# Row maxima of two heads at once: the low products in two row tiles of 64 rows, 24 steps ahead of the scores

## The chip, the cores and the metric

The kernel runs on one core of a Trainium2 chip. The metric is the device time of one execution in microseconds. An engine's own queue runs in order; PE is the matrix engine, with its weight loads shown apart as PEld, DVE the vector engine, ACT the scalar engine, POOL the general engine, SP a queue that only issues transfers.

## The reference

Attention with pooled queries, 8 batches of 8 heads, then a layer of 8 experts of which each token takes one:

```python
q_pool = q.reshape(B, H, S // factor, factor, D).mean(axis=3)          # 576 queries, D = 64
scores = scale * np.matmul(q_pool, k.transpose(0, 1, 3, 2))            # 576 x 1152
scores = scores - np.max(scores, axis=-1, keepdims=True)
attn = np.exp(scores)
attn = attn / (np.sum(attn, axis=-1, keepdims=True) + 1e-09)
attn_out = np.matmul(attn, v)
...
h = np.maximum(x[mask] @ w1[e], 0.0)
out[mask] = gate_w[mask, None] * eom[mask, e, None] * (h @ w2[e])
```

## The kernel before

Attention comes first and lasts up to some 1030 us; the experts follow. The heads go in 32 pairs (two heads of one batch). A value in float32 is kept as a high part, rounded to the form in which the matrix engine streams at full rate, and a low part, the rest. A product of queries and keys is then three products: high with high, low q with high k, and high q with low k. `qa` holds the high q in 64 rows and the low q in 64 rows below; `ka` holds the high k twice. One matmul of `ka` and `qa` thus gives the first two. `qb` and `kb` hold high q and low k in rows 0 to 63 and, in further rows, what the scores need of the row maxima; a matmul of these gives the third product.

**Scores and exponentials.** A step of the program is one chunk of 128 keys of one head: 18 steps for a pair, 576 in all. In a step the scores (`sps`, keys in the partitions, 576 queries in two halves; lines 394 and 396) are computed on PE, ACT takes their exponential twice (`ph` in float16, `p32`), and POOL or DVE makes the low part `pl`. Six steps later `av` (lines 425 to 427) multiplies with the values, mostly two chunks in every other step (`BURST`).

**Maxima.** The scores are shifted by the row maximum, which must be known earlier. So the same products are computed a second time, now with queries in the partitions (`mgen`, line 331): a pair has 1152 queries, 9 tiles of 128, of which tile 4 takes the end of head 0 and the start of head 1; each tile has three chunks of 384 keys. A chunk is two matmuls into one PSUM bank (`mp`), three for tile 4, whose third takes `kp` (low k of both heads, head 0 in rows 0 to 63, head 1 in rows 64 to 127) with `qd`, a weight matrix with zeros outside two blocks. DVE reduces each chunk to one column of `pm` (line 332). There are three banks, given out in turn (`psum`); routers and transposes use them too. After 5 and after 9 tiles the columns are reduced (`m9`), transposed on PE (line 366, in `rows`), split in high and low (lines 371 and 372) and sent by transfers on ACT's queue into `qb`.

**Order.** It is written out by hand: the loop over steps calls, in this order, what is left of the step before (`pendv`), the routers, the scores, the preparation of a later pair (`prep_at`), maxima, more preparation, `rows`, and `av`. Maxima advance 27 chunks in 18 steps, 1.5 in a step, and end `LEAD` = 18 steps before the scores that need them. The preparation (table `PREP`: loads, sums, high and low parts, transfers into `ka`, `kb`, `qa`, `qb`) is set out in thirds of a step. `prep_at` counts them from an offset of at most 9.

**Router.** Every fourth pair a batch is complete; its logits `lT` (32 rows) are transposed on PE, five times 32 by 32 (line 522 of this kernel).

Of the kernel before, what the change touches and what calls it, by code (L numbers as in the profile page):

```python
# [8 lines left out]
F32 = mybir.dt.float32  # L9
F32R = mybir.dt.float32r  # L10
# [5 lines left out]
ALU = mybir.AluOpType  # L16
AX = mybir.AxisListType
PSUM = bass.MemoryType.PSUM

LEAD = 18  # L20
L0 = 18
LS = 0
RI = 7
PREP0 = ((0, 'lk'), (6, 'qsum'), (10, 'kh', 0), (11, 'qh'), (12, 'kh', 1), (13, 'ql'), (14, 'kl'), (13, 'dq', 0), (14, 'dq', 1), (17, 'qd'), (21, 'sk', 0, 0), (24, 'sk', 0, 1), (27, 'sk', 1, 0), (30, 'sk', 1, 1), (23, 'dl', 0), (24, 'dl', 1),
        (53, 'lv'), (71, 'amax', 0), (74, 'amax', 1), (81, 'gmax'), (82, 'scale', 0), (85, 'scale', 1), (90, 'scale', 2), (93, 'vh', 0), (93, 'vs', 0), (96, 'vh', 1), (97, 'vl', 0), (100, 'vs', 1), (104, 'vl', 1))
# [24 lines left out]
NQ = 576  # L50
# [17 lines left out]
def attention(tc, qT, kT, vL, wg, keep, xrows, idscr, cum, pairs, setup, scat, init, exps):  # L68
    nc = tc.nc
    nb = len(pairs) // 4  # L70
    with ExitStack() as ctx:
# [16 lines left out]
        def psum(hold=False, name="tp"):  # L88

            while len(held) == 3:  # L90
                pop() if fill else pendv.pop(0)()
            k = next(i for i in banks if i not in held)
            free(k)
            if hold:
                held.add(k)
            x = ps_m.tile([128, 512], F32, name=name, tag=f"mp{k}")
            return (x, k) if hold else x
# [11 lines left out]
        for L, shape, name in ((KBs, [68, 2, S], "kb"), (KAs, [128, 2, S], "ka"), (QAs, [128, 2 * NQ + 64], "qa"), (QBs, [68, 2, NQ], "qb")):  # L109
            for i in order:  # L110
                L[i] = (lp if i == order[2] else ep).tile(shape, F32R, name=f"{name}{i}")
        QDs = [ep.tile([128, 128], F32R, name=f"qd{i}") for i in range(2)]
        for i in range(3):
            nc.gpsimd.memset(QAs[i].bitcast(F32)[:, NQ:NQ + 64], 0.0)
# [15 lines left out]
        def prep(n, table):  # L130
# [2 lines left out]
            b, hp = p  # L133
            ka, kb, qa, qb, vt = KAs[n % 3], KBs[n % 3], QAs[n % 3], QBs[n % 3], VTs[n % 2]
            sc = sm.tile([128, 2], F32, name="sc", bufs=4)
            states[n] = dict(ka=ka, kb=kb, qa=qa, qb=qb, vt=vt, sc=sc, p=p, n=n, qd=QDs[n % 2])
            kp = ld.tile([128, S], F32R, name=f"kp{n}", tag="kp", bufs=KPB)
            kpf = ld.tile([128, S], F32, name="kpf")
            states[n]['kp'] = kp
# [2 lines left out]
            xk = sq.tile([128, S], F32R, name=f"xk{n}", tag="xk")  # L142
            yq = sq.tile([128, NQ], F32R, name="yq")
            qs = yq.bitcast(F32)
            xq = sq.tile([128, NQ], F32R, name="xq")
            am = sm.tile([128, 2], F32, name="am")
            inv2 = sm.tile([128, 2], F32, name="inv2")
            gm = []
# [151 lines left out]
                out.setdefault(r, []).append(f)  # L300
            return out

        def mtile(t):

            if t < 4: return [(0, 128 * t)]
            if t == 4: return [(0, 512), (1, NQ)]
            return [(1, NQ + 64 + 64 + 128 * (t - 5))]

        def mgen():

            for n in range(len(pairs)):
                st = states[n]
                ka, kb, qa, qb = st['ka'], st['kb'], st['qa'], st['qb']
                qbf = qb.rearrange("p h n -> p (h n)")
                for t0, t1 in ((0, 5), (5, 9)):
                    nt = t1 - t0
                    pm = sm.tile([128, 16], F32, name="pm")
                    ch = [(t, c) for t in range(t0, t1) for c in range(3)]
                    for i, (t, c) in enumerate(ch):
                        mp = psum(name=f"mp{n}")[:, 0:384]  # L320
                        cs = slice(384 * c, 384 * c + 384)
                        ops = []
                        mt = mtile(t)
                        for (h, o) in mt:
                            ops.append((qa[:, o:o + 128], ka[:, h, cs]))
                            if len(mt) == 1:
                                ops.append((qb[0:66, h, 128 * t if h == 0 else 64 + 128 * (t - 5):][:, 0:128], kb[0:66, h, cs]))
                        if len(mt) == 2:
                            ops.append((st['qd'], st['kp'][:, cs]))
                        for j, (l, r) in enumerate(ops):  # L330
                            nc.tensor.matmul(mp, lhsT=l, rhs=r, start=j == 0, stop=j == len(ops) - 1)  # L331
                        nc.vector.tensor_reduce(out=pm[:, i:i + 1], in_=mp, axis=AX.X, op=ALU.max)  # L332
                        pop()
                        if i < len(ch) - 1:
                            yield
                    m9 = sm.tile([128, 5], F32, name="m9")

                    def ch0(m9=m9, pm=pm, nt=nt, t0=t0, t1=t1, qbf=qbf):
                        nc.vector.tensor_reduce(out=m9[:, 0:nt], in_=pm[:, 0:3 * nt].rearrange("p (t c) -> p t c", c=3), axis=AX.X, op=ALU.max)
                        pend_t.append((m9, nt, t0, t1, qbf, now[0]))  # L340
                    fill.append(ch0)
                    yield

        fill = []
# [2 lines left out]
        def pop(k=1):  # L347
            while k and fill:
                fill.pop(0)()
                k -= 1  # L350
# [9 lines left out]

        def rows(force=False):
            while pend_t and (force or now[0] >= pend_t[0][-1] + TLAG):
                m9, nt, t0, t1, qbf, _ = pend_t.pop(0)
                tp, tk = psum(True)
                tp = tp[0:nt, 0:128]
                nc.tensor.transpose(out=tp, in_=m9[:, 0:nt], identity=ident)
                mr = sm.tile([5, 2, 128], F32R, name="mr")[0:nt]
                c0 = 16.0 * SHIFT

                def split(tp=tp, tk=tk, mr=mr, qbf=qbf, t0=t0, t1=t1, nt=nt):  # L370
                    nc.vector.tensor_scalar(out=mr[:, 0], in0=tp, scalar1=c0, scalar2=None, op0=ALU.subtract)
                    nc.vector.scalar_tensor_tensor(out=mr[:, 1], in0=tp, scalar=c0, in1=mr.bitcast(F32)[:, 0], op0=ALU.subtract, op1=ALU.subtract)
                    free(tk)

                    def send():
                        for j in range(2):
                            dmaf(qbf[66 + j:67 + j, 128 * t0:128 * t1].rearrange("o (t n) -> o t n", n=128), mr[:, j], nc.scalar)
                    pendd.append((send, now[0]))
                if now[0] < 18:
                    split()  # L380
                else:
                    pendv.append(split)
# [238 lines left out]
        def adv(k, g, want):  # L621
            while pos[k] < want:
                next(g, None)
                pos[k] += 1
# [3 lines left out]
        def prep_at(s, ph):  # L628
            u = 3 * (s + SLEAD) + ph
            for n in range(max(u // 54 - 2, 0), min(u // 54 + 2, NP)):  # L630
                r = u - 54 * n + min(3 * (LEAD - 15), 2 * n)
                if r == 0:
                    preps[n] = prep(n, PREP if n > 1 else PREP0 if n else PREPF)
                if n in preps:
                    for f in preps[n].pop(r, ()):
                        f()

        E = mybir.EngineType
        with tc.manual_schedule(engines={E.PE, E.DVE, E.Activation, E.Pool}):
            for s in range(-SLEAD, 0):  # L640
                for ph in range(3):
                    prep_at(s, ph)
                if s == -RI:
                    for i in (1, 2):
                        dmaf(QBs[i][64:66], QBs[0][64:66])
                        dmaf(KBs[i][64:68], KBs[0][64:68])
                if s == 1 - SLEAD + INIT:
                    consts()
                if s == -3:
                    init(0)  # L650
                if s >= -int(L0):
                    adv('m', mg, int(1.5 * (s + 1 + L0)))
                    now[0] = s
                    sends()
                    pop(3)
                    rows()
            for s in range(18 * NP + 14):
                now[0] = s
                live = s < 18 * NP
                if s % 18 == 2 and 0 < s // 18 < 5:  # L660
                    with tc.issue_after(lastk[0].ins):
                        init(s // 18)
                sends()
                while pendv:
                    pendv.pop(0)()
                for r in routers:
                    if not s % 2 or not live or not r[1]:
                        r[1] = next(r[0], 0)
                pop()
                if live:  # L670
                    next(sg)
                prep_at(s, 0)
                mw = min(27 * NP, int(1.5 * (s + 1 + min(LEAD, L0 + LS * s))))
                if pos['m'] < mw:
                    adv('m', mg, pos['m'] + 1)
                prep_at(s, 1)
                adv('m', mg, mw)
                if s < 54 or s % 2 == 0:
                    rows()
                if pos['m'] == 27 * NP:  # L680
                    pop(2)
                j = s - ALAG
                for _ in range(BURST.get(j % 18, 0) if 0 <= j < 18 * NP else 0):
                    next(ag)
                prep_at(s, 2)
                if not live:
                    pop(3)
            pop(99)
            for r in routers:
                for _ in r[0]: pass  # L690
# [512 lines left out]
```

## Time and profile before

| | |
|---|---|
| median of 2 runs | 1527.74 us (1527.46 to 1528.02) |
| profiled execution | 1531.21 us, span from first to last instruction 1529.5 us |
| mean granted clock of the matrix engine | 0.987 |
| PE / PEld busy | 1485.5 / 1347.8 us |
| ACT / DVE / POOL busy | 1123.0 / 1106.9 / 1005.6 us |
| matmuls of the maxima (L331) | 960 of ka, 768 of kb, 96 of kp |
| reduces of the maxima (L332) | 864 of 551 ns |

Busy time of PE is the union of matmuls that overlap, each with its whole latency; the cost of one in a stream is the distance between starts, which the timeline shows. An idle time has behind it the engine and the line that is thought to have ended it. A shape such as 66*128 is rows by columns of the weights.

### The profile page before, as it was taken

Reading aid. Unit: us, or ns where it says so; the run is one execution under the profiler, and the core shown is the slowest. Engines: PE = TensorE matmul, PEld = TensorE weight load, DVE = VectorE, ACT = ScalarE, POOL = GpSimd, SP = SyncE. Lnnn points to the kernel's source line nnn. Section 1 sums busy time; section 2 is a strip of 40 time slices with the busy share of each in tenths; the row PEclk is TensorE's granted clock in tenths of the full one; section 3 lists DMA queues with packets and bytes.
Section 4 is the critical chain, followed back from the end, with each engine's and each line's share of the span. In section 5 each row is a group of like instructions: output and inputs, shape, how many; then the busy total and the mean of one; then the engine's idle time right before and its main releaser. Section 6 shows DMA issues by size and latency. Waiting matters only on the chain. (4 is left out here: it accounts for less than half of the span.)

```text
span 1529.5 us, 40884 instructions
## 1 busy us (share of the span) xinstructions
PE 1485.5 (97%) x15838; PEld 1347.8 (88%) x15838; DVE 1106.9 (72%) x2339; ACT 1123.0 (73%) x1949; POOL 1005.6 (66%) x889
## 2 busy tenths in 40 slices
PE   7999999999999999999999999979999999999998
PEld 6999999999999999999999899967888888888875
DVE  7677777776786777677777777647777777777762
ACT  5888888887888888888888888865565565565552
POOL 4887898788878888889878988766233233333210
PEclk9999999999999999999999999989999999999999
DMA  5577566665675566656765676065836666544550
GB/s 168 135 193 188 134 153 172 164 150 133 160 171 155 134 158 167 162 133 156 176 154 152 146 176 161 19 241 164 319 106 231 233 216 224 203 151 163 179 188 35
DMA packets 91984, 253.35 MB, mean 166 GB/s; under 512 B 12714, under 2 KB 16954, under 8 KB 91778
## 3 DMA queue, kind: packets, MB, share of 16 engines
q1 hardware_dynamic: 81194, 228.93, 53.5%
q0 software_dynamic: 9152, 20.85, 3.9%
q8 instruction: 129, 2.11, 0.6%
q10 hardware_dynamic: 1440, 0.89, 0.2%
q14 instruction: 69, 0.57, 0.1%
HBM read 164.23 MB, written 23.02 MB: 122 GB/s over the span
## 5 line engine op out<-in xcount | busy, mean ns | idle before, releaser
L332 DVE TENSOR_REDUCE pm<-mp 128x1 f32<-128x384 f32 x864 | 453.1, 551 | 219.5 <-PE mp L331 218.5
L410 POOL TENSOR_TENSOR pl<-p,ph 128x576 f16<-128x576 f32 x383 | 490.4, 1286 | 148.7 <-ACT ph L409 116.0
L408 ACT ACTIVATE p<-sps 128x576 f32<-128x576 f32 x383 | 250.7, 655 | 98.6 <-PE sps L396 58.8
L331 PE MATMUL mp<-ka,qa 128*128 128x384 f32 x960 | 315.1, 344 | 0.0
L425 PEld LDWEIGHTS <-ph 128*128 128x128 f16 x2880 | 263.2, 97 | 40.0 <-issue 28.9
L425 PE MATMUL av<-vt,ph 128*128 128x65 f16 x2880 | 296.4, 194 | 0.1
L426 PE MATMUL av<-vt,ph 128*128 128x64 f16 x2880 | 294.2, 195 | 0.0
L427 PE MATMUL av<-vt,pl 128*128 128x65 f16 x2880 | 293.3, 193 | 0.0
L394 PE MATMUL sps<-qa,ka 128*128 128x288 f32 x1152 | 279.8, 325 | 13.4 <-DVE pl L404 6.6
L426 PEld LDWEIGHTS <-ph 128*128 128x128 f16 x2880 | 265.9, 97 | 0.8
L427 PEld LDWEIGHTS <-pl 128*128 128x128 f16 x2880 | 266.1, 99 | 0.0
L331 PE MATMUL mp<-kb,qb 66*128 66x384 f32 x768 | 260.9, 340 | 0.9 <-DVE kb L205 0.6
L409 ACT ACTIVATE ph<-sps 128x576 f16<-128x576 f32 x383 | 249.4, 651 | 0.0
L396 PE MATMUL sps<-qb,kb 68*128 68x288 f32 x1152 | 248.6, 298 | 0.0
L905 PE MATMUL hps<-x,w1h 128*128 128x512 f32 (+1 forms) x704 | 233.3, 393 | 6.7 <-DVE x L889 4.2
L394 PEld LDWEIGHTS sps<-qa,ka 128*128 128x128 f32 x1152 | 185.0, 192 | 18.2 <-ACT ph L409 9.0
L396 PEld LDWEIGHTS sps<-qb,kb 68*128 68x128 f32 x1152 | 187.4, 191 | 0.0
L331 PEld LDWEIGHTS mp<-ka,qa 128*128 128x128 f32 x960 | 178.7, 190 | 1.8 <-DVE pm L332 1.5
L907 ACT COPY hs<-hps 128x512 f32<-128x512 f32 (+1 forms) x88 | 49.1, 558 | 174.0 <-PE hps L905 174.0
L905 PE MATMUL hps<-x,w1l 128*128 128x256 f32 (+1 forms) x704 | 167.0, 279 | 0.0
L404 DVE TENSOR_TENSOR pl<-sps,ph 128x576 f16<-128x576 f32 x193 | 145.9, 756 | 20.1 <-ACT sps L401 18.3
L400 ACT ACTIVATE ph<-sps 128x576 f16<-128x576 f32 x193 | 126.4, 655 | 41.1 <-PE sps L396 30.8
(231 smaller groups left out, 2948.0 us busy)
## 6 DMA issues: line engine op xcount, KB each, us to landing
ka<-xk SPq DMA_DIRECT2D x120, 288.0 KB
raw1b<-in_w_dram SPq DMA_DIRECT2D x24, 1024.0 KB
raw2b<-in_w_dram SPq DMA_DIRECT2D x24, 1024.0 KB
raw1a<-in_w_dram SPq DMA_DIRECT2D x22, 1024.0 KB
raw2a<-in_w_dram SPq DMA_DIRECT2D x22, 1024.0 KB
vp<-in_vL_dram SPq DMA_DIRECT2D x32, 576.0 KB
qp<-in_qT_dram SPq DMA_DIRECT2D x31, 576.0 KB
kpf<-in_kT_dram SPq DMA_DIRECT2D x31, 576.0 KB
```

The costliest lines, as they stand in the source:

```text
L331: nc.tensor.matmul(mp, lhsT=l, rhs=r, start=j == 0, stop=j == len(ops) - 1)
L332: nc.vector.tensor_reduce(out=pm[:, i:i + 1], in_=mp, axis=AX.X, op=ALU.max)
L394: nc.tensor.matmul(sps[:, j, 0:288], lhsT=ka[:, h, ks], rhs=qa[:, o + 288 * j:o + 288 * j + 288], start=True, stop=False)
L396: nc.tensor.matmul(sps[:, j, 0:288], lhsT=kb[:, h, ks], rhs=qb[:, h, 288 * j:288 * j + 288], start=False, stop=True)
L404: nc.vector.tensor_tensor(out=pl.rearrange("p (j n) -> p j n", j=2), in0=x, in1=ph2, op=ALU.subtract)
L408: nc.scalar.activation(out=p32.rearrange("p (j n) -> p j n", j=2), in_=x, func=AF.Exp, scale=1.0 / 16)
L409: e_ = nc.scalar.activation(out=ph2, in_=x, func=AF.Exp, scale=1.0 / 16)
L410: nc.gpsimd.tensor_tensor(out=pl, in0=p32, in1=ph, op=ALU.subtract)
L425: nc.tensor.matmul(av_[:, qb, 0:65], lhsT=hi, rhs=vt[:, h, c, 0:65], start=c == 0 and qb == 0, stop=False)
L426: nc.tensor.matmul(av_[:, qb, 0:64], lhsT=hi, rhs=vt[:, h, c, 66:130], start=False, stop=False)
L427: nc.tensor.matmul(av_[:, qb, 0:65], lhsT=lo, rhs=vt[:, h, c, 0:65], start=False, stop=c == NC - 1 and qb == 4)
L905: nc.tensor.matmul(hp[:, f, 0:n], lhsT=W1[l][g][:, c, fs], rhs=d['x'][:, c, 0:n], start=c == 0 and l == 0, stop=c == 3 and l == 0)
```

## The change

From the second pair on, the maxima of tile t of head 0 and tile t of head 1 are computed together, into two banks: first the product of `ka` and `qa` for head 0, then for head 1, each of 128 rows; then the product of high q and low k for head 0 from rows 0 to 63 of `xq` and `kp`, and for head 1 from rows 64 to 127 of the same tiles. These two are tiles of 64 rows by 128 columns at row 0 and row 64. `xq`, high q of both heads as `kp` has low k, becomes double buffered. Tile 4 stays as it was. The first pair keeps the old form.

A pair has then 15 events (12 double tiles and 3 single ones of tile 4). A table, `EVENTS`, sets the steps: from 24 before the pair's scores to 7 before, one event in a step and none at the 7th, 11th and 17th; the single ones stand 3rd, 9th and 15th of the 18. The second pair has a table of its own. The 9 columns of maxima are closed once for a pair: one reduce, one transpose, two sends. The preparation up to the transfers starts earlier (`OFFA`, 21 thirds of a step at most), the preparation of the values keeps its place.

```diff
-LEAD = 18
 L0 = 18
-LS = 0
+OFFA = (0, 2, 14, 20, 21)
+EVENTS = tuple(-24 + i for i in range(18) if i not in (6, 10, 16))
+EVENT1 = (-18, -17, -16, -15, -14, -13, -13, -12, -11, -11, -10, -9, -9, -8, -7)
...
+        XQs = [sq.tile([128, NQ], F32R, name=f"xq{i}") for i in range(2)]
...
+                for i in range(15):
+                    t, c = (4, i // 5) if i % 5 == 2 else divmod(i - (i + 2) // 5, 3)
+                    cs = cols[c]
+                    if t == 4:
                         mp = psum(name=f"mp{n}")[:, 0:384]
...
+                        both(mp, cs)
+                        reduce(pm, 12 + c, mp)
+                    else:
+                        o = (128 * t, 64 + 128 * t)
+                        mp = [psum(name=f"mp{n}")[:, 0:384] for _ in range(2)]
+                        for h in range(2):
+                            nc.tensor.matmul(mp[h], lhsT=qa[:, h * o1 + o[h]:h * o1 + o[h] + 128], rhs=ka[:, h, cs], start=True, stop=False)
+                        for h in range(2):
+                            r = slice(64 * h, 64 * h + 64)
+                            nc.tensor.matmul(mp[h], lhsT=xq[r, o[h]:o[h] + 128], rhs=kp[r, cs], start=False, stop=True)
+                        for h in range(2):
+                            reduce(pm, 3 * (5 * h + t) + c, mp[h])
+                    if i == 14:
+                        closing(pm, 9, 0, qbf)
                     yield
...
-                r = u - 54 * n + min(3 * (LEAD - 15), 2 * n)
-                if r == 0:
+                ra, rv = u - 54 * n + OFFA[min(n, 4)], u - 54 * n + min(9, 2 * n)
+                if ra == 0:
                     preps[n] = prep(n, PREP if n > 1 else PREP0 if n else PREPF)
                 if n in preps:
-                    for f in preps[n].pop(r, ()):
-                        f()
+                    for r in (ra,) if ra < 50 else (rv,) if rv >= 50 else ():
+                        for f in preps[n].pop(r, ()):
+                            f()
...
+        steps = [18 * n + e for n in range(1, NP) for e in (EVENTS if n > 1 else EVENT1)]
...
-                mw = min(27 * NP, int(1.5 * (s + 1 + min(LEAD, L0 + LS * s))))
-                if pos['m'] < mw:
+                for _ in range(steps.count(s)):
                     adv('m', mg, pos['m'] + 1)
                 prep_at(s, 1)
-                adv('m', mg, mw)
```

On PE, two steps of the 18th pair's scores before (numbers behind a name tell the buffers apart; `sps` are scores, `mp` maxima, the weighted sums `av` begin with the last row):

```order
L394 MATMUL sps_12214<-qa_123,ka_120 128x288 x2
L396 MATMUL sps_12214<-qb_126,kb_117 128x288 x2
L331 MATMUL mp_12225<-ka_121,qa_124 128x384
L331 MATMUL mp_12225<-kb_118,qb_127 128x384
L331 MATMUL mp_12229<-ka_121,qa_124 128x384
L331 MATMUL mp_12229<-kb_118,qb_127 128x384
L394 MATMUL sps_12240<-qa_123,ka_120 128x288 x2
L396 MATMUL sps_12240<-qb_126,kb_117 128x288 x2
L331 MATMUL mp_12249<-ka_121,qa_124 128x384
L331 MATMUL mp_12249<-kb_118,qb_127 128x384
L425 LDWEIGHTS ph
```

The same two steps of the changed kernel, whose lines 421 and 423 are the scores, 361 the full products, 364 the products of 64 rows and 452 the weighted sums:

```order
L421 MATMUL sps_12073<-qa_123,ka_120 128x288 x2
L423 MATMUL sps_12073<-qb_126,kb_117 128x288 x2
L361 MATMUL mp_12084<-ka_121,qa_124 128x384
L361 MATMUL mp_12085<-ka_121,qa_124 128x384
L364 MATMUL mp_12084<-kp_11080,xq_129 128x384
L364 MATMUL mp_12085<-kp_11080,xq_129 128x384
L421 MATMUL sps_12102<-qa_123,ka_120 128x288 x2
L423 MATMUL sps_12102<-qb_126,kb_117 128x288 x2
L361 MATMUL mp_12111<-ka_121,qa_124 128x384
L361 MATMUL mp_12112<-ka_121,qa_124 128x384
L364 MATMUL mp_12111<-kp_11080,xq_129 128x384
L364 MATMUL mp_12112<-kp_11080,xq_129 128x384
```

Three chunks into three banks, one after the other, became four chunks into two banks at a time; behind the first group stand scores, behind the second the weighted sums.

On PE, where the maxima of a pair are transposed, before (line 366, at the end of the first five tiles, ahead of the weighted sums):

```order
L331 MATMUL mp_12490<-ka_121,qa_124 128x384
L331 MATMUL mp_12490<-kb_118,qb_127 128x384
L366 MATMUL tp<-ident,m_12388 5x128
L425 LDWEIGHTS ph
L425 MATMUL av_12253<-vt_140,ph 128x65
```

And now (line 393, once for a pair, behind a single tile of the next pair, which is `both` in line 319):

```order
L319 MATMUL mp_12416<-ka_122,qa_125 128x384 x2
L319 MATMUL mp_12416<-kp_11744,qd_132 128x384
L393 MATMUL tp<-ident,m_12319 9x128
L452 LDWEIGHTS ph
L452 MATMUL av_12119<-vt_142,ph 128x65
```

The transpose has 9 rows instead of 5 and 4; the second one of a pair is gone.

More of the change, by code (lines that the diff above doesn't have):

```diff
@@ L135, in prep @@
             sc = sm.tile([128, 2], F32, name="sc", bufs=4)
-            states[n] = dict(ka=ka, kb=kb, qa=qa, qb=qb, vt=vt, sc=sc, p=p, n=n, qd=QDs[n % 2])
+            xq = XQs[n % 2]
+            states[n] = dict(ka=ka, kb=kb, qa=qa, qb=qb, vt=vt, sc=sc, p=p, n=n, qd=QDs[n % 2], xq=xq)
             kp = ld.tile([128, S], F32R, name=f"kp{n}", tag="kp", bufs=KPB)
@@ L144, in prep @@
             qs = yq.bitcast(F32)
-            xq = sq.tile([128, NQ], F32R, name="xq")
             am = sm.tile([128, 2], F32, name="am")
@@ L301, in prep, with reduce, closing, ch0 @@
             return out
[L303 to L307, printed above, removed]
+        def reduce(pm, i, mp):
+            nc.vector.tensor_reduce(out=pm[:, i:i + 1], in_=mp, axis=AX.X, op=ALU.max)
+            pop()
+        def closing(pm, nt, t0, qbf):
+            m9 = sm.tile([128, 9], F32, name="m9")
+            def ch0():
+                nc.vector.tensor_reduce(out=m9[:, 0:nt], in_=pm[:, 0:3 * nt].rearrange("p (t c) -> p t c", c=3), axis=AX.X, op=ALU.max)
+                pend_t.append((m9, nt, t0, qbf, now[0]))
+            fill.append(ch0)
+        def group(mp, *ops):
+            for j, (l, r) in enumerate(ops):
+                nc.tensor.matmul(mp, lhsT=l, rhs=r, start=j == 0, stop=j == len(ops) - 1)
         def mgen():
@@ L312, in mgen @@
                 st = states[n]
-                ka, kb, qa, qb = st['ka'], st['kb'], st['qa'], st['qb']
+                ka, kb, qa, qb, kp, xq = (st[x] for x in ('ka', 'kb', 'qa', 'qb', 'kp', 'xq'))
                 qbf = qb.rearrange("p h n -> p (h n)")
[L315 to L319, printed above, removed]
-                        mp = psum(name=f"mp{n}")[:, 0:384]
[L321 to L341, printed above, removed]
@@ new lines, in mgen, with both @@
+                o1 = NQ + 64
+                def both(mp, cs):
+                    group(mp, (qa[:, 512:640], ka[:, 0, cs]), (qa[:, NQ:NQ + 128], ka[:, 1, cs]), (st['qd'], kp[:, cs]))
+                cols = [slice(384 * c, 384 * c + 384) for c in range(3)]
+                if n == 0:
+                    for t0, t1 in ((0, 5), (5, 9)):
+                        pm = sm.tile([128, 32], F32, name="pm")
+                        for i in range(3 * (t1 - t0)):
+                            t, cs = t0 + i // 3, cols[i % 3]
+                            mp = psum(name="mp0")[:, 0:384]
+                            if t == 4:
+                                both(mp, cs)
+                            else:
+                                h, o = (0, 128 * t) if t < 4 else (1, 64 + 128 * (t - 5))
+                                group(mp, (qa[:, h * o1 + o:h * o1 + o + 128], ka[:, h, cs]), (qb[0:66, h, o:o + 128], kb[0:66, h, cs]))
+                            reduce(pm, i, mp)
+                            if i < 3 * (t1 - t0) - 1:
+                                yield
+                        closing(pm, t1 - t0, t0, qbf)
+                        yield
+                    continue
@@ new lines, in mgen @@
+                pm = sm.tile([128, 32], F32, name="pm")
+                for i in range(15):
+                    t, c = (4, i // 5) if i % 5 == 2 else divmod(i - (i + 2) // 5, 3)
+                    cs = cols[c]
+                    if t == 4:
+                        mp = psum(name=f"mp{n}")[:, 0:384]
+                        both(mp, cs)
+                        reduce(pm, 12 + c, mp)
+                    else:
+                        o = (128 * t, 64 + 128 * t)
[9 more added lines that the diff above has]
+                        closing(pm, 9, 0, qbf)
@@ L362, in rows @@
             while pend_t and (force or now[0] >= pend_t[0][-1] + TLAG):
-                m9, nt, t0, t1, qbf, _ = pend_t.pop(0)
+                m9, nt, t0, qbf, _ = pend_t.pop(0)
                 tp, tk = psum(True)
@@ L366, in rows, with split @@
                 nc.tensor.transpose(out=tp, in_=m9[:, 0:nt], identity=ident)
-                mr = sm.tile([5, 2, 128], F32R, name="mr")[0:nt]
+                mr = sm.tile([9, 2, 128], F32R, name="mr")[0:nt]
                 c0 = 16.0 * SHIFT
-                def split(tp=tp, tk=tk, mr=mr, qbf=qbf, t0=t0, t1=t1, nt=nt):
+                def split(tp=tp, tk=tk, mr=mr, qbf=qbf, t0=t0, t1=t0 + nt):
                     nc.vector.tensor_scalar(out=mr[:, 0], in0=tp, scalar1=c0, scalar2=None, op0=ALU.subtract)
@@ L672, in attention @@
                 prep_at(s, 0)
-                mw = min(27 * NP, int(1.5 * (s + 1 + min(LEAD, L0 + LS * s))))
-                if pos['m'] < mw:
+                for _ in range(steps.count(s)):
                     adv('m', mg, pos['m'] + 1)
                 prep_at(s, 1)
-                adv('m', mg, mw)
                 if s < 54 or s % 2 == 0:
                     rows()
-                if pos['m'] == 27 * NP:
+                if s > steps[-1]:
                     pop(2)
```

## The prediction, made before the changed kernel ran

> **What bounds the kernel now.** I read the page first (engine table and clock), then the table by stretches of time, then the groups of the maxima, and last the timeline of the matrix engine around single matmuls. The page:
>
> ```profile
> PE 1485.5 (97%) x15838; PEld 1347.8 (88%) x15838; DVE 1106.9 (72%) x2339; ACT 1123.0 (73%) x1949; POOL 1005.6 (66%) x889
> ...
> PEclk9999999999999999999999999989999999999999
> ```
>
> ```profile
> 400.00:600.00 200.00, 198.13 (x2703) 187.07 (x2702) 150.28 (x381) 170.13 (x315) 170.72 (x151) 1.00 0.60 151
> 600.00:800.00 200.00, 198.13 (x2696) 187.48 (x2693) 149.80 (x373) 170.41 (x316) 167.73 (x147) 1.00 0.64 158
> 950.00:986.00 36.00, 36.00 (x488) 34.30 (x487) 27.22 (x67) 29.79 (x55) 26.60 (x24) 1.00 0.17 45
> 986.00:1017.00 31.00, 26.31 (x402) 24.16 (x401) 9.74 (x22) 26.18 (x46) 25.09 (x19) 0.89 0.39 139
> ```
>
> The columns after the length are busy us of PE, PEld, DVE, ACT and POOL. In the attention's steady part PE is busy 198 of 200 us at full clock; ACT and POOL have 30 us in 200 to spare, DVE 50. In that stage whatever PE needs more or less goes into the time one for one. From 986 us on there are no maxima left, and PE is idle for 5 of 31 us.
>
> The share of the change:
>
> ```profile
> L331 PE MATMUL mp<-ka,qa 128*128 128x384 f32 x960 | 315.1, 344 | 0.0
> L331 PE MATMUL mp<-kb,qb 66*128 66x384 f32 x768 | 260.9, 340 | 0.9 <-DVE kb L205 0.6 <-ACT kb L207 0.3
> L332 DVE TENSOR_REDUCE pm<-mp 128x1 f32<-128x384 f32 x864 | 453.1, 551 | 219.5 <-PE mp L331 218.5
> L366 PE MATMUL tp<-ident,m 128*5 128x128 f32 x64 | 17.5, 273 | 0.9 <-DVE m L339 0.7
> L394 PE MATMUL sps<-qa,ka 128*128 128x288 f32 x1152 | 279.8, 325 | 13.4 <-DVE pl L404 6.6 <-ACT ph L409 6.5
> L522 PE MATMUL tp<-ident,lT 32*128 32x32 f32 x40 | 4.1, 227 | 0.3 <-DVE lT L501 0.3
> ```
>
> The means (344, 340 ns) are latencies and overlap. What a matmul costs in a stream is the distance from start to start, which the timeline of PE gives (start, duration):
>
> ```profile
> 502.60 0.34 PE L331 MATMUL mp<-ka,qa 128*128 128x384 f32 x1
> 502.77 0.34 PE L331 MATMUL mp<-kb,qb 66*128 66x384 f32 x1
> 502.94 0.34 PE L331 MATMUL mp<-ka,qa 128*128 128x384 f32 x1
> 503.12 0.34 PE L331 MATMUL mp<-kb,qb 66*128 66x384 f32 x1
> 503.29 0.42 PE L394 MATMUL sps<-qa,ka 128*128 128x288 f32 x2
> ```
>
> Two maxima tiles are four matmuls from 502.60 to 503.29: 0.69 us, **0.173 us each**. The product with 66 rows costs as much as the one with 128. That is what the change aims at: 12 double tiles in each of 31 pairs, 372 in all, whose two low products are to run side by side.
>
> **What going into a row tile costs.** This kernel has one place with a matmul of few rows, the 32-row transposes of L522 (shape 32*128), between maxima and scores:
>
> ```profile
> 301.40 0.34 PE L331 MATMUL mp<-ka,qa 128*128 128x384 f32 x1
> 301.57 0.33 PE L331 MATMUL mp<-kb,qb 66*128 66x384 f32 x1
> 301.83 0.49 PE L522 MATMUL tp<-ident,lT 32*128 32x32 f32 x5
> 302.26 0.53 PE L394 MATMUL sps<-qa,ka 128*128 128x288 f32 x2
> 302.63 0.43 PE L396 MATMUL sps<-qb,kb 68*128 68x288 f32 x2
> ```
>
> ```profile
> 301.40 0.19 PEld L331 LDWEIGHTS mp<-kb,qb 66*128 66x128 f32 x1
> 301.83 0.38 PEld L522 LDWEIGHTS tp<-ident,lT 32*128 32x128 f32 x5 [0.24 <-DVE r L435]
> 302.26 0.30 PEld L394 LDWEIGHTS sps<-qa,ka 128*128 128x128 f32 x2
> ```
>
> Elsewhere the weights of the next matmul are loaded while the last one streams (the load at 301.40 starts with the matmul at 301.40). Here the load and the first 32-row matmul start together at 301.83, **0.26 us** after the last full matmul and not 0.173. The five transposes pass at (0.49 - 0.227) / 4 = 0.066 us, so the last starts at 302.09; the scores' load begins 0.17 us later, again with its matmul, and the two L394 take 0.53 us where the pair at 503.29 took 0.42: **0.11 us** of weight load in the open. I read this as the array running empty before it changes to a row tile and before it changes back. The release named in brackets (DVE, L435) is a guess of the trace; the 0.26 speaks against it, since a wait for another engine would not fit the end of the stream so well.
>
> Of the 40 transposes most take 222 ns, the first of a group 244:
>
> ```profile
> L522 PE MATMUL tp<-ident,lT x40: 221/222/244, 178.1 to 1024.0; 32*128 32x32 f32 x40
> ```
>
> A narrow tile the other way shows nothing of the kind:
>
> ```profile
> 309.39 0.34 PE L331 MATMUL mp<-kb,qb 66*128 66x384 f32 x1
> 309.58 0.27 PE L366 MATMUL tp<-ident,m 128*4 128x128 f32 x1
> 309.68 0.19 PE L425 MATMUL av<-vt,ph 128*128 128x65 f16 x1
> 309.71 0.19 PE L426 MATMUL av<-vt,ph 128*128 128x64 f16 x1
> ```
>
> Four columns of weights come 0.19 us after the matmul before. So it is rows, not columns, that the 0.26 belongs to. The Trainium skill, "TensorEngine Tiling (Array Packing)", section Key Properties, says that a change of tiling mode, not just of the tile, drains the engine: the 0.26 agrees with it, and if L366's narrow load counts as a mode of that page, its 0.19 doesn't.
>
> **The sum for one double tile.** Before: 0.69. After: full product of head 0, 0.173; head 1, then 0.26 until the first 64-row load; that load in the open, 0.11; the second 64-row matmul behind the first by a distance d; 0.26 until the load of what follows; its load in the open, 0.11 before scores or a router's float32 matmul, 0.03 before the weighted sums (the distance 309.68 to 309.71). By the table of steps 9 of the 12 double tiles of a pair stand in odd steps, where scores or a router follow, and 3 in even steps, where the weighted sums follow.
>
> The load going in isn't in the trace: 0.02 if it hides as L522's did (0.244 - 0.222), 0.11 if it is like L394's. It is a float32 load of 128 columns for a plain product, as L394's, so 0.11. For d the bounds are 0 (both at once) and 0.173 (not side by side at all); the only two row-tiled matmuls in a row, L522's, are 0.066 apart, and I take that.
>
> - followed by float32: 0.173 + 0.26 + 0.11 + 0.066 + 0.26 + 0.11 = 0.98, that is +0.29
> - followed by float16: 0.90, that is +0.21
> - mean (9 x 0.29 + 3 x 0.21) / 12 = +0.27; times 372: **+100 us**
>
> The Trainium skill, "TensorE: Matmul & The Clock Gate", Part 3 (the mechanism), puts concurrent row tiles some 4 ns apart. By it d is 0.004 and the term 0.062 x 372 = 23 us smaller; no run shown here has two row tiles at once.
>
> **The other parts.** One closing reduce, one transpose and two sends for a pair instead of two, two and four. Of these only the transpose is on PE: 31 x 0.10 (309.58 to 309.68) = -3 us; the DVE and ACT parts lie beside PE. The maxima end 24 steps before the scores and not 18, so the last 24 steps have none. The row 986 to 1017 shows that such steps don't wait for PE, so taking maxima out of six more steps gives nothing back, while their work (6 x 1.5 tiles x 2 x 0.173) joins earlier steps: +3 us. A longer PE lets ACT and DVE get ahead, so part of the 13.4 us that L394 waited for them goes: -5 us, half or less since some of it stands after 986. The prep's loads come earlier by up to four steps, and the first double tile follows the last loads of qa by about four steps instead of six (about 1.7 us a step: 558 steps up to 986 us); the transfers run beside PE and I cost this at nothing. If one were late, PE would wait for it once a pair, 31 times; 1 us each would be 31 us. The three single tiles (head 0's end with head 1's start, three full matmuls) keep their cost.
>
> Sum: 100 - 3 + 3 - 5 = +95 us. The profiled execution took 1531.21 us with a span of 1529.5; the runs' median is 1527.74, 0.2% less, so the sum is simply put on the median: 1622 us, 6% slower. Bounds: with the first load hidden and d = 0 a double tile costs +0.13 or +0.05, mean 0.11, 42 us, with the other parts 1565; with d = 0.173 it is +0.38, 140 us, 1663. A few us of difference are nothing against the 2% (31 us) that counts here as no change.
>
> **The rivals.**
>
> *No drain for tiles of 64 rows (faster).* L522 has 32 rows and is a transpose; the L366 row shows that a partial tile need not cost anything. Then a double tile is 3 x 0.173 plus d: 0.52 to 0.59 instead of 0.69, -0.10 to -0.17, 38 to 64 us off: 1464 to 1490, say 1478. ACT and POOL, at 170 of 200, would let a pair shrink that far. The point from which it decides: in and out together may cost 0.10 us before the gain is gone; L522 shows about 0.39 (twice 0.09 and twice 0.11). Against it stands that row; I give 0.13. The same Trainium skill page on tiling, section Theoretical Speedup, puts up to a factor of two on contractions of 64 rows or less; the rival is what that would bring here.
>
> *Drain, but no load in the open.* If both loads are done while the array empties, a double tile is 0.173 + 0.26 + 0.03 + 0.26 = 0.72, +0.03, 12 us: 1540. For it: L522's first load cost 0.02. Against it: the 0.11 at L394 on the way out. The same band holds the case that the 64-row matmuls are not placed as tiles at all and run like full ones: no switch, four times 0.173, no change. Together 0.07.
>
> *Banks.* A double tile takes two of the three banks of the maxima at once, and a reduce holds one for 0.55 us. Three times in a pair two double tiles stand with only scores between (the first place shown ahead): four banks within some 1.5 us of PE. If DVE is then behind, PE waits up to one reduce, 93 x 0.55 = 51 us on top of the forecast: 1673. Against it: DVE has 50 us in 200 free, and its 219.5 us idle at L332 are waits for PE. It decides when the first reduce ends over 1.5 us after its tile began. 0.08.
>
> **How the numbers follow.** Forecast (switches drain, loads partly in the open, side by side or nearly) 0.72; banks on top 0.08; loads hidden or no tiles 0.07; no drain 0.13. Slower by over 2% (above 1558): 0.72 + 0.08 = 0.80; within 2%: 0.07; faster: 0.13. The range leaves out the fast rival and the far end of the banks, and takes in the bounds 1565 and 1663 with most of the way down to the second rival: 1545 to 1662.
>
> **What the changed profile would show.** The first 64-row matmul starts 0.26 us after head 1's full product, its load with it: right; 0.17: the drain is absent. The distance of the two 64-row matmuls gives d: under 0.03 they are loaded and run side by side, at 0.17 they aren't. The scores behind a double tile start with their load, as at 302.26, and their first pair takes 0.53. DVE, ACT and POOL are less busy in each 200 us of the attention (ACT about 154 for 170), and PE's stretch of 200 us remains full. PE waiting at the maxima's line for DVE's reduces would be the rival of the banks. The forecast is wrong if row tiles of 64 switch without emptying the array.

## The result, and the profile after

The changed kernel takes 1800.07 us (median of 2 runs, 1795.76 to 1804.38) against 1527.74: 1.178 times the time before, interval 1.166 to 1.190. The direction was forecast, the size was not: +272 us where +95 stood.

The page of the changed kernel (line 306 is the reduce of the maxima, 361 the full products of a double tile, 364 the products of 64 rows):

```profile
PE 1637.2 (91%) x15807; PEld 1334.9 (74%) x15807; DVE 1089.8 (61%) x2246; ACT 1121.0 (62%) x1949; POOL 1002.6 (56%) x889
PEclk9898899999899988889999998989899999999999
L306 DVE TENSOR_REDUCE pm<-mp 128x1 f32<-128x384 f32 x864 | 444.5, 552 | 504.5 <-PE mp L364 492.4
L361 PE MATMUL mp<-ka,qa 128*128 128x384 f32 x744 | 219.4, 367 | 108.4 <-DMA qa<-yq 70.1
L364 PE MATMUL mp<-kp,xq 64*128 64x384 f32 x744 | 173.9, 464 | 0.0
```

PE is no longer full, and its clock has dips. The table by stretches of time (busy us of PE, PEld, DVE, ACT, POOL, then the granted clock) says the same of the steady part:

```profile
400.00:600.00 200.00, 178.38 (x2081) 142.85 (x2081) 112.62 (x273) 131.68 (x245) 130.86 (x114) 0.92 0.52 124
600.00:800.00 200.00, 176.12 (x1954) 142.01 (x1951) 106.46 (x259) 124.38 (x232) 124.65 (x110) 0.87 0.47 110
```

No other engine has come near its limit; all are idler than before. So PE waits, and the list of who waited for whom (us in total, times, longest) names what for:

```profile
PE mp L361 <- DMA qa<-yq: 70.1, 33, 4.5
PE mp L361 <- DMA kb<-kp: 27.0, 16, 3.3
```

97 us of waits for transfers, once or twice a pair. The maxima of the double tiles don't read `kb`; its transfers stand in the same queue, between the two into `qa`, and the list names a wait after the transfer that seems to have ended it. One pair's first events on PE's timeline, and the clock in three stretches around them:

```profile
486.69 0.43 PE L421 MATMUL sps<-qa,ka 128*128 128x288 f32 x2
486.95 0.43 PE L423 MATMUL sps<-qb,kb 68*128 68x288 f32 x2
490.59 0.41 PE L361 MATMUL mp<-ka,qa 128*128 128x384 f32 x1 [3.21 <-DMA qa<-yq]
492.45 0.66 PE L361 MATMUL mp<-ka,qa 128*128 128x384 f32 x1 [1.45 <-DMA qa<-yq]
493.04 0.69 PE L364 MATMUL mp<-kp,xq 64*128 64x384 f32 x2
```

```profile
480.00:486.00 6.00, 6.00 (x89) 5.06 (x87) 4.04 (x9) 4.94 (x12) 4.66 (x6) 1.00 0.98 214
486.00:498.00 12.00, 7.34 (x52) 5.30 (x52) 3.22 (x8) 4.09 (x8) 1.93 (x2) 0.72 0.53 132
498.00:520.00 22.00, 21.73 (x274) 17.69 (x275) 14.21 (x34) 16.85 (x29) 17.99 (x15) 1.00 0.28 71
```

Head 0's product waits 3.21 us, head 1's 1.45 more, and then the clock is low for a while: head 1's product of 384 columns, 0.34 us elsewhere, takes 0.66, and the two of 64 rows 0.69 instead of 0.44. This comes back with nearly every pair. Over the whole execution the mean clock is 0.940 where it was 0.987, so (1 - 0.940) x 1793.9 = 108 us worth of clock are missing instead of 20.

The queue SP shows when the data set out. The two transfers of low q into `qa`, before and after (start, duration of the issue):

```profile
485.67 0.54 SPq L126 DMA_DIRECT2D qa<-yq  x1
488.81 0.46 SPq L126 DMA_DIRECT2D qa<-yq  x1
```

```profile
483.91 0.46 SPq L128 DMA_DIRECT2D qa<-yq  x1
486.39 0.46 SPq L128 DMA_DIRECT2D qa<-yq  x1
```

The first of each two is head 0's, the second head 1's. Head 1's now goes out at 486.39, and PE reaches the event that needs both at 487.38 (490.59 - 3.21), behind the scores. Before, head 1's `qa` was first read by chunk 12 of its pair, eight steps after the maxima began; now the very first event reads both heads'.

The times of issue, of landing and of the first reader, as medians over the 31 pairs, say it for both halves. Before, head 0's transfer was issued 9.0 us ahead of its first reader and took 5.7 us to land; head 1's was issued 19.4 us ahead and took 4.1. Now PE reaches the first event 5.1 us after head 0's issue and 2.9 us after head 1's, and both take 6.6 us. So neither half is there in time: PE idles 63 us ahead of the first products of head 0 and 45 us ahead of those of head 1.

The tiles themselves, on the same timeline:

```profile
501.64 0.45 PE L364 MATMUL mp<-kp,xq 64*128 64x384 f32 x2
502.02 0.53 PE L421 MATMUL sps<-qa,ka 128*128 128x288 f32 x2
502.39 0.43 PE L423 MATMUL sps<-qb,kb 68*128 68x288 f32 x2
502.66 0.52 PE L361 MATMUL mp<-ka,qa 128*128 128x384 f32 x2
503.10 0.44 PE L364 MATMUL mp<-kp,xq 64*128 64x384 f32 x2
```

Two products of 64 rows together take 0.44 or 0.45 us, as long as a single one (0.44, shown below): they run side by side. Over all 372 double tiles the median distances from start to start are 0.268 us from head 1's full product to the first of 64 rows, 0.003 from it to the second, and 0.37 to what follows.

### The profile page after: what moved, and what is told of

It reads as the page before. It is cut to its first block, busy times and chain, and to the rows that moved or that the text cites. A ratio compares the mean times of both kernels' runs of the same rounds, so it can differ in the third digit from the quotient of the medians.

```text
span 1793.9 us, 40456 instructions
## 1 busy us (share of the span) xinstructions
PE 1637.2 (91%) x15807; PEld 1334.9 (74%) x15807; DVE 1089.8 (61%) x2246; ACT 1121.0 (62%) x1949; POOL 1002.6 (56%) x889
## 5 line engine op out<-in xcount | busy, mean ns | idle before, releaser
L306 DVE TENSOR_REDUCE pm<-mp 128x1 f32<-128x384 f32 x864 | 444.5, 552 | 504.5 <-PE mp L364 492.4
L361 PE MATMUL mp<-ka,qa 128*128 128x384 f32 x744 | 219.4, 367 | 108.4 <-DMA qa<-yq 70.1
L452 PE MATMUL av<-vt,ph 128*128 128x65 f16 x2880 | 316.9, 199 | 0.8 <-DVE xb L463 0.8
L453 PE MATMUL av<-vt,ph 128*128 128x64 f16 x2880 | 314.8, 200 | 0.0
L454 PE MATMUL av<-vt,pl 128*128 128x65 f16 x2880 | 314.0, 198 | 0.0
L421 PE MATMUL sps<-qa,ka 128*128 128x288 f32 x1152 | 304.4, 347 | 8.9 <-DVE pl L431 6.3
L452 PEld LDWEIGHTS <-ph 128*128 128x128 f16 x2880 | 274.2, 100 | 40.5 <-issue 32.1
L454 PEld LDWEIGHTS <-pl 128*128 128x128 f16 x2880 | 278.4, 102 | 0.0
L453 PEld LDWEIGHTS <-ph 128*128 128x128 f16 x2880 | 277.8, 101 | 0.7
L361 PEld LDWEIGHTS mp<-ka,qa 128*128 128x128 f32 x744 | 133.1, 201 | 128.4 <-issue 92.8
L364 PE MATMUL mp<-kp,xq 64*128 64x384 f32 x744 | 173.9, 464 | 0.0
```

The costliest lines, as they stand in the source:

```text
L361: nc.tensor.matmul(mp[h], lhsT=qa[:, h * o1 + o[h]:h * o1 + o[h] + 128], rhs=ka[:, h, cs], start=True, stop=False)
L364: nc.tensor.matmul(mp[h], lhsT=xq[r, o[h]:o[h] + 128], rhs=kp[r, cs], start=False, stop=True)
L421: nc.tensor.matmul(sps[:, j, 0:288], lhsT=ka[:, h, ks], rhs=qa[:, o + 288 * j:o + 288 * j + 288], start=True, stop=False)
L452: nc.tensor.matmul(av_[:, qb, 0:65], lhsT=hi, rhs=vt[:, h, c, 0:65], start=c == 0 and qb == 0, stop=False)
L453: nc.tensor.matmul(av_[:, qb, 0:64], lhsT=hi, rhs=vt[:, h, c, 66:130], start=False, stop=False)
L454: nc.tensor.matmul(av_[:, qb, 0:65], lhsT=lo, rhs=vt[:, h, c, 0:65], start=False, stop=c == NC - 1 and qb == 4)
```

## The experiments

Each was timed beside the kernel before on its chip (1529.8 to 1530.43 us there, 1527.74 for the result above); "us" are medians. All the numbers of theories in the expectations are from before the run.

**Preparation three steps earlier.**

```diff
-OFFA = (0, 2, 14, 20, 21)
+OFFA = (0, 2, 14, 26, 30)
```

> The changed kernel with the preparation of queries and keys nine thirds of a step earlier (three steps, OFFA 30 instead of 21 from the fifth pair on), row tiles and events as they are. Theory A (late transfers: PE waits some 100 us for qa, the gaps halve the clock for some 200 us, which costs some 90 us, and the row tiles themselves cost 85 us): the waits for qa go under 15 us, the mean clock returns to 0.98 or more, the time is about 1610 us. Theory B (the tiles of 64 rows make the array look idle and so halve the clock): the waits go, but the clock stays near 0.94 and the time near 1700 us.

Measured: 1645.42 us, ratio 1.078 (1.073 to 1.082), clock 0.988. What PE still waits for:

```profile
PE av L454 <- POOL pl L437: 11.4, 8, 5.4
...
PE mp L361 <- DMA qa<-yq: 6.0, 2, 4.5
```

The waits for `qa` went down to 6 us and the clock came back with 372 row tiles still in the program: theory B falls. It took 155 us off. The time is 35 us above theory A's; 11 of them are a new wait, for POOL, that the earlier preparation brings, and the rest stays open here.

**No row tiles, everything else as changed.**

```diff
-                            nc.tensor.matmul(mp[h], lhsT=xq[r, o[h]:o[h] + 128], rhs=kp[r, cs], start=False, stop=True)
+                            nc.tensor.matmul(mp[h], lhsT=qb[0:66, h, o[h]:o[h] + 128], rhs=kb[0:66, h, cs], start=False, stop=True)
```

> The changed kernel with its events and its preparation as they are, but the low products taken from kb and qb as full matmuls of 66 rows, so that no row tile is left in the maxima. Theory A: the waits for qa remain (90 us or more, now also for kb), the clock stays near 0.94, the time falls by the tiles' 85 us to about 1715 us. Theory B: the clock returns to 0.98, about 1630 us.

Measured: 1811.40 us, ratio 1.184 (1.180 to 1.188), clock 0.916.

```profile
PE mp L361 <- DMA qa<-yq: 95.1, 35, 5.5
PE mp L361 <- DMA kb<-kp: 46.2, 22, 5.4
```

Without a single row tile in the maxima the time is no better, and the clock is lower: the waits and the clock are not of the tiles. Theory A missed the time by 96 us. In these two lines the waits are 141 us for 97, and (1 - 0.916) x 1810.7 = 152 us worth of clock are missing for 108, so the tiles' price didn't come off. A PE that is quicker reaches the same transfers earlier; but the low products now also need `kb`, which is issued last, and the run doesn't tell the two reasons apart.

**Both edits.** 

> Both edits: no row tiles, and the preparation nine thirds earlier. Both theories: no waits, full clock, about the time of the kernel before (1525 to 1535 us); against the run with early preparation alone the difference is the price of the row tiles, 85 us by theory A (372 tiles of 0.23 us).

Measured: 1614.54 us, ratio 1.057 (1.053 to 1.060). A miss for both theories: with neither tiles nor more than 7 us of waits for `qa` it is still 85 us above before. Against the first experiment the row tiles cost 31 us and not 85. Two waits are long; of the first the kernel before had none, of the second 6.6 us:

```profile
PE av L453 <- POOL pl L436: 16.9, 10, 6.5
PE sps L420 <- DVE pl L430: 14.4, 28, 1.1
```

**Events two steps later.**

```diff
-EVENTS = tuple(-24 + i for i in range(18) if i not in (6, 10, 16))
+EVENTS = tuple(-22 + i for i in range(18) if i not in (6, 10, 16))
```

> The changed kernel with the events two steps later (22 steps ahead of the scores instead of 24), preparation and row tiles as they are. Theory A: the transfers get 3.5 us more, which is about what PE waited in a pair, so most of the waits go (under 40 us), the clock is 0.97 or more, about 1630 us. Theory B: clock near 0.94, 1700 us or more.

Measured: 1764.46 us, ratio 1.153 (1.147 to 1.159), clock 0.956.

```profile
PE sps L423 <- DMA qb<-mr: 52.0, 27, 2.5
```

A miss for theory A in time (1630) and clock (0.97); the time alone would fit theory B, which the first two experiments exclude. The waits for `qa` are down to 2 us, and a new one took their place: the scores now wait for their own maxima (`mr` into `qb`). The events have no room to move later, since the maxima are sent only behind the last of them.

**Transfers of another pair.** To take the waits away without moving anything, the maxima read the `qa` of the pair before, which landed long ago; the shift of the scores then comes from other queries.

```diff
+                qa = states[max(n - 1, 0)]['qa']
```

> The changed kernel whose maxima read the qa of the pair before (which has long landed) instead of their own, so that their shift is that of another pair's queries; every instruction, its shape and its place stay. Theory A (late transfers and the clock behind them are all but the tiles' price): no waits for qa, half clock under 40 us, time 1528 + 85 for the tiles + some 10 at the start = 1615 to 1630 us. Rival C (the order of events itself costs steadily, since the two early runs without waits for qa still lay 85 us above theory): 1645 us or more.

Measured: 1626.29 us, ratio 1.062 (1.058 to 1.067), clock 0.990. The steady part:

```profile
400.00:600.00 200.00, 197.79 (x2475) 160.03 (x2474) 133.12 (x320) 156.36 (x289) 155.92 (x135) 1.00 0.59 141
```

PE is full again at full clock, and the time is in theory A's band, under rival C's. **The late `qa`, with all that follows from it, costs 1800 - 1626 = 174 us.**

**The same without row tiles.** Here qa, qb and kb are those of the pair before, and the low products have 66 rows as in the second experiment. 

> The same with qa, qb and kb of the pair before and full matmuls of 66 rows for the low products: the events' order alone, with neither row tiles nor late transfers. Theory A: 1530 to 1545 us. Rival C: 1570 us or more. The difference to the run with row tiles is the tiles' price: 85 us from the distances (372 x 0.23), or 30 to 40 if PE's extra time again hides other waits.

Measured: 1588.54 us, ratio 1.039 (1.033 to 1.045): above theory A, for rival C. The order of events costs some 58 us by itself in this run, so the fifth experiment's 96 us are not the 85 for tiles and 10 for the start that theory A put there. Part of the 58 can be named:

```profile
PE sps L423 <- DMA qb<-mr: 9.0, 7, 2.5
PE mp L362 <- DMA ka<-xk: 8.0, 7, 2.3
...
PE tp L393 <- DVE lT L528: 5.4, 20, 0.5
```

The tiles add 38 us to it, not the 85 of their distances, as was held possible. A quicker PE meets waits that a slower one doesn't: it idles 60 us here and 43 with the tiles. These 17 us are a part of the difference of 47; the rest isn't shown.

**Transfers into qa first.**

```diff
-(26, 'ql'), (29, 'qd'), (30, 'dl', 0), (32, 'dl', 1),
+(26, 'ql'), (29, 'qd'), (27, 'dl', 0), (28, 'dl', 1), (31, 'db', 0), (33, 'db', 1),
```

where `db` holds the transfers into `qb` and `kb` that stood in `dq` and `dl`. 

> The changed kernel, row tiles and events as they are, with the transfers into qa put ahead of those into qb and kb (which the maxima don't read): the low q goes out at thirds 27 and 28 instead of 30 and 32, and qb and kb after it. Theory A: the last transfer is issued some 3 us earlier and finds a shorter queue, so the waits for qa fall from 97 us to under 40 and the half clock from 201 us to under 100: 1650 to 1710 us. If the waits were set by the preparation on POOL and not by the queue: no change, 1800 us.

Measured: 1668.84 us, ratio 1.091 (1.085 to 1.097), clock 0.978.

```profile
PE mp L368 <- DMA kb<-kp: 13.6, 8, 3.3
PE mp L368 <- DMA qb<-xq: 5.9, 10, 2.1
PE mp L368 <- DMA qa<-yq: 4.3, 8, 1.1
```

As theory A has it: 131 us come back from the order and the step of these transfers alone, with the preparation on POOL where it was.

**Single tiles in the old order.** In the kernel before, each low product becomes one matmul of 64 rows, two of them never next to each other:

```diff
+                            if len(mt) == 1 and n:
+                                r, o_ = slice(64 * h, 64 * h + 64), 128 * t if h == 0 else 64 + 128 * (t - 5)
+                                ops.append((st['xq'][r, o_:o_ + 128], st['kp'][r, cs]))
```

> The kernel before with its own order, where from the second pair on each low product is one matmul of 64 rows from xq and kp instead of 66 rows from qb and kb, alone in its row tile: 744 goes into a row tile and back, nothing side by side, no late transfers. From the distances of the changed kernel (0.268 in, 0.370 out, 0.11 of load, less 0.352; 0.08 less before float16) 0.37 us each, 275 us: about 1800 us. If a switch costs less when no second tile follows: below 1700 us.

Measured: 1774.66 us, ratio 1.160 (1.154 to 1.166), clock 0.988. On the timeline (line 335 is now all maxima):

```profile
501.53 0.33 PE L335 MATMUL mp<-ka,qa 128*128 128x384 f32 x1
501.79 0.44 PE L335 MATMUL mp<-kp,xq 64*128 64x384 f32 x1
502.16 0.27 PE L370 MATMUL tp<-ident,m 128*4 128x128 f32 x1
```

The expectation was 275 us more, about 1800 us; it is 244. On the timeline it is 0.26 in and 0.37 out, as with two. (1774.66 - 1530.43) / 744 = 0.33 us for going in and out once, with no late transfer anywhere: the switch is shown by itself, near the 0.37 of the distances.

**Work in place of the wait.** Ahead of the first double tile of a pair:

```diff
+                        if i == 0:
+                            o_ = states[n - 1]
+                            for _ in range(16):
+                                nc.tensor.matmul(mp[0], lhsT=o_['qa'][:, 0:128], rhs=o_['ka'][:, 0, cs], start=True, stop=True)
```

> The changed kernel with 16 full matmuls more ahead of the first double tile of every pair from the second on; they write the bank that the tile then overwrites, from the qa and ka of the pair before, and need no transfer. 31 x 16 x 0.177 = 88 us of work more on PE. Theory A (the waits halve the clock, and the halves cost some 90 us beside the waits): PE is busy while the transfers land, the half clock falls from 201 us to under 80, the waits from 108 us to under 40, and the time falls to 1700 to 1740 us although work was added. Rival D (only the waits cost, the half clock lies inside idle time): the work fills the waits, and the time stays at 1790 to 1810 us.

Measured: 1758.30 us, ratio 1.149 (1.143 to 1.155), clock 0.984.

```profile
PE mp L365 <- DMA qa<-yq: 22.5, 17, 2.0
PE mp L365 <- DMA kb<-kp: 8.9, 8, 1.8
```

The run has 88 us more work on PE and takes 42 us less. The clock is back (0.984), the waits are down to 31 us. Rival D falls. The time lies 18 us above theory A's band; presumably the filler delays where a wait was shorter than its 2.8 us, which isn't shown.

**Both low products in one row tile.**

```diff
-                            r = slice(64 * h, 64 * h + 64)
+                            r = slice(0, 64)
```

> The run that reads the qa of the pair before (1626 us), with both low products of a double tile taken from rows 0 to 63, that is in the same row tile, so that they can't run side by side; head 1's maxima then lack their own low product. If running side by side saves what the distance of 3 ns says, the second product now comes 0.17 to 0.18 us after the first, 372 x 0.174 = 65 us more: about 1690 us. If it saves less, since a wait elsewhere takes the time: 1640 us.

Measured: 1661.17 us, ratio 1.086 (1.081 to 1.091), 35 us more than with two tiles.

```profile
505.24 0.61 PE L365 MATMUL mp<-kp,xq 64*128 64x384 f32 x2
505.78 0.55 PE L508 MATMUL tp<-ident,xb 128*128 128x128 f32 x3
```

The two now end 0.61 us after the first began and not 0.44. The median distances are 0.279 between them and about 0.26 to what follows: 0.17 a double tile, 62 us in all, of which 35 reach the time, between the two expectations. PE's idle time shrinks by 7 us (36 for 43); where the rest went isn't shown. So side by side does save the 0.17 that the change wanted, and that is less than the 0.33 of the switch.

## Why the prediction was wrong

*The failed step* is the one among the other parts on the preparation: "the transfers run beside PE and I cost this at nothing. If one were late, PE would wait for it once a pair, 31 times; 1 us each would be 31 us." Transfers were late with nearly every pair, by 97 us in all, and the low clock behind the waits came on top. The slack was counted in steps and not read from the trace before, which had it. Of head 0's 9.0 us the transfer itself took 5.7, and the two steps that the prediction took away are 3.4 us (2 x 1.7): nothing was left. The "four steps" from the last load of `qa`, some 7 us, were 2.9. And the prediction overlooked that head 1's half was needed eight steps later in the old order and at once in the new; the old order of tiles, head 0's first, says so.

*What was not in the sum at all* is the clock. The prediction assumed it full. The changed kernel's trace has 214 us at half clock; in 34 of them PE was idle, and half of the other 180, 90 us, is lost. In the run without late transfers it is 33 us with 7 idle, 13 lost. The difference of 77 us and the 97 us of waits make the 174 measured. That the clock follows from the waits is shown from three sides: waits taken away with the tiles kept (0.990), tiles taken away with the waits kept (0.916), and work put into the waits (0.984).

*The sum for the rest came out, in part by luck.* Without late transfers the changed kernel takes 1626 us, where 1622 was forecast; but that agreement has errors on both sides. For a double tile ahead of scores 0.98 us was summed; the distances give 0.177 + 0.268 + 0.003 + 0.370 + 0.11 = 0.93. The way in (0.26) and the loads in the open (the 0.370 is 0.26 and the 0.11 of the load going in, since the matmul's start is that of its load) were right. The distance d was 0.003 and not 0.066; the 4 ns that the Trainium skill, "TensorE: Matmul & The Clock Gate", Part 3, gives for it agree. The tiles' price in the time was smaller still, 38 us where 100 stood. Against that, the order of events costs more than the 3 us it was given. In the run without late transfers and tiles it is 58 us, and where all of it goes is not settled: the waits named there are 22 us, PE idles 60 us in all instead of 31, and from the first scores to those of the second pair it takes 43 us instead of 34.

*The rivals.* No drain: excluded, by 0.268 at 372 places and by the single tiles. Loads hidden: excluded by the 0.11. Banks: the list of waits of the run without late transfers (line 362 is its full products) has

```profile
PEld mp L362 <- DVE pm L306: 10.3, 39, 0.5
```

so a reduce does hold weight loads (PEld) up now and then, for 10 us of the 51 that were the bound; the matmuls themselves wait for one for 0.6 us.

*What the changed profile showed of the list at the end:* 0.26 in, d under 0.03, the first scores pair at 0.53 as said. "PE's stretch of 200 us remains full" was wrong (178 of 200), and that was the sign of the failed step. ACT has 132 of 200 and not 154; without late transfers it has 156.

## What to carry to other kernels

A reordering that starts a consumer with both halves of its data moves the deadline of the half that came last, and starting it earlier eats the slack of the other: compare each transfer's issue, and the time it takes to land, with its own first reader. Waits of a few microseconds on a full matrix engine can cost nearly twice their length where the clock follows them, here 174 us for 97. And when a part is made cheaper or taken out, the waits behind it may take up what it saved: price a part in a run in which nothing else is late.

## What the runs showed of the hardware that was not expected

The changed kernel has 28 places where PE idled 2.2 us or more in total, in pieces at most 6 us apart; most are the waits of the first event. At 27 of them the clock fell to half, for 3.4 to 13.7 us; at 1309 us, among the experts, an idle time of 2.27 us left it full. Of shorter idle times some brought it (1.63 us at 1052) and some didn't (2.19 us at 896). The Trainium skill, "TensorE: Matmul & The Clock Gate", Part 1, puts the return to half rate behind an idle window of about 3.4 us; at 12 of the 27 places the longest single idle time was under 2 us, and once it was 1.1.

Two row tiles of 64 rows start 3 ns apart and end together, with their weight loads side by side as well. Two matmuls in the same row tile are 0.279 us apart where full ones are 0.176. The weight loads of that run (start, duration, both loads merged) show why:

```profile
505.24 0.29 PEld L365 LDWEIGHTS mp<-kp,xq 64*128 64x128 f32 x2 [0.26 <-issue]
```

By the medians the second load starts 0.108 us after the first, and its matmul 0.172 us after it. So the second load was hidden behind the first product, as between full matmuls; the 0.279 holds the first load, which stood in the open.
